# Mamba-2 scan and maxout FFN on one core: output products of five chunks in 512 columns and turned on VectorE, masks in 32x32 tiles, a new order

## The chip, the cores and the metric

The kernel runs on one core of one Trainium2 chip. The metric is the device time of one execution in microseconds (us). The kernel before was timed three times; where one figure is given, it is the median.

## The reference

A state-space scan with decay feeds a feed-forward layer whose activation is the largest of three products. All data are float32.

```python
# x (4, 8, 768, 32)   a (4, 8, 768)   B, C (4, 8, 768, 16): batch, head, position, ...
log_a = np.log(np.clip(a, 1e-06, 1.0))
for c in range(768 // 32):
    cum = np.cumsum(la, axis=-1)                       # la: log_a of these 32 positions
    L = np.exp(cum[:, :, :, None] - cum[:, :, None, :]) * causal
    y_intra = np.einsum('bhij,bhjd->bhid', np.einsum('bhin,bhjn->bhij', Cc, Bc) * L, xc)
    y_inter = np.einsum('bhin,bhnd->bhid', Cc, state) * np.exp(cum)[:, :, :, None]
    y[:, :, sl] = y_intra + y_inter
    state = decay_full * state + sum_j(B_j x_j * decay_from_j)
# bridge: (batch, head, position, 32) -> (batch * position, head * 32) = (3072, 256)
h = np.maximum(np.maximum(x @ w1, x @ w2), x @ w3)      # w1, w2, w3 (256, 768)
return h @ w_out                                        # w_out (768, 256)
```

## The kernel before

**Chunks.** The 768 positions are cut into six chunks c of 128; a chunk has its four batches side by side, so an activation tile has 512 columns (tokens), and 128 rows of features. The scan of a chunk needs the state left by the chunk before. All of it is in SBUF; weights and inputs are loaded once.

**Steps and the order.** The program is a table of some 1,500 named steps. Each belongs to an engine (t TensorE = PE, v VectorE = DVE, a ScalarE = ACT, p GpSimd = POOL, s SyncE = SP, whose steps are DMAs), lists the tiles it uses, and issues a few instructions. One hand-written string, `ORDER`, names the steps, `name` or `name/engine`; the program walks it once, so that on each engine the instructions stand in that order, and waits between engines follow from the tiles. A tile gets a slot of its pool at its first use and gives it back after its last. There are eight slots of PSUM (`ps`, one bank of 128x512 each).

**Precision.** A float32 product is taken as three products of parts, H·H, H·L and L·H (z = 0, 1, 2), where H is a rounded copy and L the rest. The weights are brought into a form for this by the steps `d` (load), `ab`, `lo`, `cl`, `sh`, `pl`, `sg`, `df`, and `h`/`l` with the name of a weight.

**The scan of a chunk.** `lB`, `lC` (loads of 32 KB) and `tB`, `tC` (32x32 transposes on DVE), or loads of 256 KB turned on PE (`trB`, `trC`), give B and C by state; `bt`/`tk` and `bk` turn B back. `s` are the products C·B, `left` and `right` are rows for the decay, and `e` or `em` multiplies them out: the exponent of L for a batch, 128 positions times eight heads of 64, one bank `e.c.b`. Of chunks 0 to 3 the causal mask is added in the same bank, by a matmul of a mask with an identity ahead of it (`mm.c.b`, `mask_mm`); `em` then accumulates onto it with two products of 32x64 tiles per batch. `xp` is the Exp into L, `w` the product with `s`, `yo` and `yw` the output y of the chunk, `A` and `S` the new state.

**The FFN of a chunk.** Chunks 0 and 1 take w1, w2, w3 in `up` steps (six matmuls of 512 columns each), with `m` and `h` for the maximum. The pairs of chunks (2, 3) and (4, 5) share products by the steps `q1` to `q7` on four banks E, F, G, H, with `x1`, `g7`, `e2`, `mx`, `hb`, `c1`, `c2`, `ha` and more around them. Either way there are six tiles of activations h (f = 0 to 5) per chunk, in parts `hH` and `hL`. Two more terms `y0`, `y1` come from y itself by a folded weight `fo`.

**The output.** A chunk's output is the sum of 24 steps `dn.c.term.z`: term h0 to h5, y0, y1, times z. Each is four matmuls, one for each batch b: the weights are the 128 tokens of the batch out of the activation tile, and 256 columns of w_out (`wo`) stream past. They add up in two banks `o.c.0` and `o.c.1`, tokens on partitions and 256 output columns per batch. `ob.c.u` copies a bank to SBUF (u = 0 on DVE, u = 1 on ACT, unless the order names another), `st.c.u` stores it, 256 KB. Chunk 5's copies and stores are in halves.

**The names in the profile.** `L892` is the matmul of `dn`, L337 the mask, L358 the `e` products, L799 `up`, L818 `q`, L506 `s`, L530 `yw`, L453 the turning back `tk`, L407 the transposes `tB` and `tC`, L184 a copy on ACT, L186 one on DVE, L189 a two-operand instruction, L402 the 32 KB loads, L650 weight loads, L955 the stores.

Of the kernel before, what the change touches and what calls it, by code (L numbers as in the profile page):

```python
# [23 lines left out]
a.1/s ident sel4 ones warm.20 own d.04 ind warm.4 ident16 table rowsel anew a.0/a clip.0 a.2  # L24
ln.0 nind scan.0 lo.04 pt0.0 pd1.0 mask mm.1.0 mm.0.0 ab.04 warm.21 pt1.0 left.0 clip.1 ln.1
mm.0.2 spread.0 warm.19 minus1 minus0 clip.2 esel En.0 d.12 warm.17 scan.1 ltC.0 pt0.1 lt.0
pd1.1 warm.11 ab.12 d.14 spread.1 mm.0.1 warm.8 cl.04 sh.04 cl.12 warm.13 warm.5 em.0.0 ln.2
scan.2 pt0.2 parity pd1.2 lo.12 lx.0 d.24 lt.1 mm.0.3 pt1.1 left.1 right.1.0 xp.0.0 d.22 sh.12
pl.12 E.0 em.0.1 xp.0.2 trC.0 cq.0.0 xp.0.3 trB.0 cpB.0 pt1.2 right.1.1 left.2 cq.0.1 xp.0.1
bd.0 ce.0 s.0 right.1.2 ab.14 cl.14 warm.18 sh.14 ltC.1 w.0.3 lo.14 w.0.2 d.02 warm.9 lo.24  # L30
En.3 warm.0 A.0 w.0.1 En.1 pl.14 ab.24 warm.10 w.0.0 lx.1 S.0.1 warm.16 d.11 lB.5.2 sg.14
sg.12 E.1 lB.2.2 lB.3.1 pl.04 lB.3.2 yw.0.0 S.0.0 yo.0 yw.0.1 mm.1.3 sg.04 E.3 cl.24 yH.0.1.1
d.10 mm.1.1 yH.0.0.1 yH.0.1.0 mm.1.2 yH.0.0.0/v yL.0.0.0 warm.23 right.2.1 right.2.0 ab.22
lC.4.7 df.04/v lC.5.6 trB.1 sh.24 yL.0.1.0 h.up04 d.00 lo.22 yL.0.1.1 right.2.2 yL.0.0.1 cl.22
l.up04/v em.1.0 xp.1.0 bt.2 cpB.1 xp.1.1 so.0.1 sa.0.1 sh.22 h.b4 pl.24 sg.24 ab.02 lC.3.3
trC.1 cq.1.0/v ce.1 lC.3.6 cq.1.1 En.2 em.1.1 lB.2.3 xp.1.3 pl.22 xp.1.2 l.b4 up.0.5.0 cl.02
df.24/v sh.02 bd.1/v up.0.4.0 E.2 sg.22 h.up24 s.1 m.0.4 w.1.1 d.01 d.21 so.1.0 lo.02 lC.2.1
A.1 S.1.0 mm.2.1 w.1.3 w.1.2 lB.2.5 l.up24 w.1.0 m.0.5 ab.11 lC.2.6 sa.1.0 warm.3 lB.2.7
up.0.4.1 mm.2.2 h.0.4 lC.3.5 yo.1 lB.4.1 S.1.1 pl.02 df.22 mm.2.3 sg.02 lC.2.0 right.3.0
h.up22 l.up22 df.02/v h.up02 l.up02 yw.1 yH.1.0.0/v up.0.5.1 yH.1.0.1/v yL.1.0.1 d.20 em.2.1  # L40
yH.1.1.1/v up.0.2.1 right.3.1 yH.1.1.0/v ab.01 lC.2.5 lC.5.0 yL.1.1.1 lB.3.3 xp.2.2 up.0.2.0
cl.11 ab.10/v lC.2.2 cl.10 lo.01 lB.2.0 yL.1.1.0 yL.1.0.0 up.1.4.0 lo.21 lC.2.3 ab.00 cl.00
xp.2.3 sh.00 ab.21 lo.11 sh.11 mm.3.0 lo.00 sw.2.0 sw.2.1 h.0.5 pl.11 sg.11 lC.4.5 mm.3.3
sh.10 sw.4.0 lo.10 mm.2.0 pl.00 ab.20/v pl.10 sw.4.1 sw.4.3 cl.01 mm.3.2 sg.10 em.2.0 m.0.2
sg.00 up.1.4.1 xp.2.1 lo.20 sh.01 xp.2.0 m.1.4 up.1.2.0 up.1.5.0 m.1.5 sw.2.2 h.0.2 h.1.4
df.00/v cl.20 sh.20 up.1.2.1 d.o2 pl.01 bt.1 sg.01 m.1.2 so.1.1/v pl.20 right.4.2 lC.2.7 h.b2
sg.20 h.up00/v lo.o2 lC.5.7 mm.3.1 l.up00 lC.2.4 df.20/v h.up20 up.0.3.0 lB.2.4 m.0.3
right.3.2 lB.2.6 em.3.1 em.3.0 d.o4 lB.2.1 l.up20 tC.2 cm.2.0 up.0.0.0.1 xp.3.0 cl.21 sh.21
pl.21 ab.o2 l.b2 up.0.3.1 tB.2 lC.4.2 sa.1.1 sg.21 xp.3.1 lC.3.4 lB.4.7 cl.o2 cm.2.1 xp.3.3
up.0.0.0.0 h.0.3 lB.3.6 tk.2 hH.0.3 h.1.2 bk.2 up.1.0.0 df.01/v d.o0 df.21 h.up21 l.up21/v  # L50
bt.0 ab.o4 lB.5.7 s.2 m.1.0 sw.2.3 lB.3.4 h.b0 lC.3.1 m.0.0 lo.o4 lB.5.3 sw.1.0 sh.o2 xp.3.2
up.0.0.1.0 up.0.0.1.1 so.2.0/v w.2.0 h.up01 w.2.1 lC.3.0 lx.2 up.1.5.1 pl.o2 sg.o2 sw.4.2
ab.o0 cd.2 h.1.5 w.2.2 hH.0.2 lC.3.2 hL.0.2 w.2.3 l.up01 cl.o0 cl.o4 sh.o4 sw.0.2 up.1.3.0
lt.3 sh.o0 lo.o0 A.2 pl.o0 up.1.3.1 S.2.0 h.wo2 lB.3.7 hH.1.2 m.1.3 S.2.1 sa.2.0 h.ss2 h.1.3
up.1.1.0 l.b0 pl.o4 l.wo2/v up.0.1.0 sw.0.0 lC.3.7 yo.2 m.1.1 sg.o0 up.1.1.1 sg.o4 hH.0.4
m.0.1/v h.0.0 lB.5.6 h.wo0 l.wo0 tC.3 cm.3.0 yw.2 yS.2.1.0 yS.2.1.1 lC.4.1 hH.1.5/v lC.5.2
h.wo4/v fold.2 lB.3.0 hH.0.5 fold.0 dn.0.h5.0 l.wo4 dn.0.h4.1 yS.2.0.1/v fold.4 right.5.1
yH.2.1.0 yH.2.1.1 bd.3 yL.2.1.1 hH.0.0 h.1.1 yS.2.0.0 yL.2.1.0 dn.0.h5.1 so.2.1/v hL.0.3
right.5.0 lB.4.2 h.fo dn.0.h2.1 hH.1.3/v yH.2.0.1 lB.3.5 tB.3 l.fo yL.2.0.1 dn.0.h0.1
# [964 lines left out]
```

## Time and profile before

| | |
|---|---|
| three runs | 239.13, 237.35, 238.9 us; median 238.9 us |
| span of the profiled execution | 236.7 us (its own time is not recorded apart; the median stands 2.2 us above its span) |
| PE | busy 221.5 us, 94% of the span, 3020 matmuls |
| DVE | busy 185.1 us, 78% |
| ACT | busy 98.6 us, 42% |
| POOL | busy 88.3 us, 37% |
| DMA | 17.49 MB in 71,051 packets, mean 74 GB/s; read 13.76 MB, written 3.15 MB |
| chain that ended last | PE 75%, DMA 9%, SP's queue 6%, ACT 4%, DVE 3% |

The span runs from the first to the last instruction of the profiled execution; the chain is the sequence of work and waits that ended last, followed back from the end. A matmul's busy time includes its way through the array, so that matmuls in a row overlap, and the pace of a row is read from its starts or from the length of many.

### The profile page before, as it was taken

How to read it: one execution, taken by the hardware profiler on the slowest of the kernel's cores; microseconds unless marked ns; L12 is line 12 of the kernel's file. 1: busy time of each engine (PE TensorE's matmuls, PEld its weight loads, DVE VectorE, ACT ScalarE, POOL GpSimd, SP SyncE). 2: the span in 40 equal slices, each digit the busy share in tenths (PEclk: the TensorE clock that was granted, in tenths of full speed). 3: DMA queues.
4: the chain of work that ended last, by engine and by line, in shares of the span. 5: the costliest groups of instructions: out<-in, count | busy, mean ns of one | idle time of the engine just before them, and what ended most of it. 6: DMA issues, size and time to landing. Idle time of an engine off the chain costs nothing.

```text
span 236.7 us, 7069 instructions
## 1 busy us (share of the span) xinstructions
PE 221.5 (94%) x3020; PEld 182.3 (77%) x3020; DVE 185.1 (78%) x340; ACT 98.6 (42%) x196; POOL 88.3 (37%) x85
## 2 busy tenths in 40 slices
...
GB/s 165 171 193 165 190 148 133 115 96 207 192 104 47 93 52 3 6 61 0 96 141 103 47 3 0 7 4 3 0 130 5 0 0 3 0 0 3 0 127 142
DMA packets 71051, 17.49 MB, mean 74 GB/s; under 512 B 63724, under 2 KB 68588, under 8 KB 71020
## 3 DMA queue, kind: packets, MB, share of 16 engines
...
q8 instruction: 24, 0.39, 0.8%
...
q14 instruction: 7, 0.06, 0.1%
HBM read 13.76 MB, written 3.15 MB: 71 GB/s over the span
## 4 chain that ended last, share of the span: by engine, by line
PE 75%; DMA 9%; SPq 6%; ACT 4%; DVE 3%; issue 1%; ACTq 0%; DVEq 0%
PE o L892 30%; PE E L818 11%; PE u L799 9%; DMA raw<-in_moe_w_dram 7%; PE G L818 6%; PE H L818 3%; PE F L818 3%; PE y L530 2%; SPq L650 2%; SPq L332 2%; PE s L506 2%; PE fold L768 2%; PE y L518 2%; DMA rawB<-in_B_dram 2%; PE A L491 1%
## 5 line engine op out<-in xcount | busy, mean ns | idle before, releaser
L189 POOL TENSOR_TENSOR u<-u,r 128x512 uint32<-128x512 uint32 (+1 forms) x12 | 12.8, 1075 | 25.1 <-DVE u L660 20.5
L189 POOL TENSOR_TENSOR hL<-x,hH 128x512 fp32r<-128x512 f32 x6 | 8.3, 1397 | 35.0 <-PE G L818 14.6
L385 ACT ACTIVATE L<-e 128x512 f32<-128x512 f32 x24 | 13.8, 595 | 6.7 <-PE e L358 6.7
L189 DVE TENSOR_TENSOR L<-s,L 128x512 f32<-128x512 f32 x24 | 15.5, 682 | 0.0
L184 ACT COPY x<-E 128x512 f32<-128x512 f32 x11 | 6.4, 586 | 16.1 <-PE E L818 15.8
L184 ACT CAST hH<-x 128x512 fp32r<-128x512 f32 x9 | 5.5, 625 | 16.8 <-DVE x L860 16.8
L189 POOL TENSOR_TENSOR hL<-h,hH 128x512 fp32r<-128x512 f32 x8 | 11.5, 1460 | 2.6 <-PE fold L768 1.3
L189 DVE TENSOR_TENSOR yL<-y,yH 128x256 fp32r<-128x256 f32 x24 | 9.6, 417 | 3.4 <-ACT yH L184 2.2
L189 DVE TENSOR_TENSOR x<-F,x 128x512 f32<-128x512 f32 x12 | 8.1, 686 | 5.0 <-PE F L818 5.0
L189 DVE TENSOR_TENSOR g<-E,g 128x512 f32<-128x512 f32 x12 | 8.3, 691 | 4.8 <-PE E L818 4.3
L189 POOL TENSOR_TENSOR T<-yS,T 128x512 f32<-128x512 f32 x3 | 4.3, 1425 | 20.0 <-PE o L892 18.3
L530 PEld LDWEIGHTS y<-L,x 64*32 64x32 f32 x768 | 8.7, 105 | 2.9 <-issue 2.2
L530 PE MATMUL y<-L,x 64*32 64x64 f32 x768 | 10.1, 224 | 0.7 <-issue 0.7
L189 DVE TENSOR_TENSOR g<-H,g 128x512 f32<-128x512 f32 x12 | 8.2, 686 | 2.8 <-ACT g L184 1.6
L184 ACT CAST yH<-y 128x256 fp32r<-128x256 f32 x17 | 5.7, 393 | 10.7 <-DVE yS L186 8.0
L877 DVE SCALAR_TENSOR_TENSOR hL<-g,hH 128x512 fp32r<-128x512 f32 x12 | 9.1, 774 | 0.9 <-PE o L892 0.9
L184 ACT COPY yS<-y 128x256 f32<-128x256 f32 x13 | 4.3, 376 | 13.1 <-PE y L530 11.6
L186 DVE COPY ob<-o 128x512 f32<-128x512 f32 (+1 forms) x5 | 3.1, 636 | 8.0 <-ACT ob L184 6.9
L184 ACT COPY ob<-o 128x512 f32<-128x512 f32 (+1 forms) x9 | 4.3, 519 | 11.9 <-PE o L892 11.9
L365 POOL TENSOR_SCALAR_AFFINE_SELECT L<-L 64x1024 f32<-64x1024 f32 x8 | 9.1, 1149 | 0.2
L662 ACT ACTIVATE r<-raw 128x512 f32<-128x512 uint32 (+1 forms) x12 | 6.4, 562 | 5.6 <-DMA raw<-in_moe_w_dram 5.6
L506 PE MATMUL s<-CT,BT 32*64 32x128 f32 x384 | 7.3, 278 | 1.5 <-ACT CT L442 1.5
...
## 6 DMA issues: line engine op xcount, KB each, us to landing
...
```

What stands on the lines that cost most here:

```text
L184: nc.scalar.copy(out=to, in_=src)
L189: engines[e].tensor_tensor(out=to, in0=p, in1=q, op=op)
L332: lambda e, c=c, p=p: engines[e].dma_start(out=at("right%d" % (c % 2))[4 * p + 3::RT], in_=at("left")[p::4, c * P:(c + 1) * P]))
L365: nc.gpsimd.affine_select(out=part, in_=part, pattern=[[0, 2 * NH], [1, Q]], compare_op=ALU.is_ge, fill=0.0, base=0, channel_multiplier=-1)
L385: lambda e, c=c, b=b: nc.scalar.activation(at("L.%d" % c)[:, b], at("e.%d.%d" % (c, b)), AF.Exp))
L506: nc.tensor.matmul(out=at("s.%d.%d" % (c, r))[side(g), b], lhsT=at("BT.%d" % c)[rows(r), b, side(g)], rhs=at("CT2.%d" % c)[rows(r), b, :, ...
L530: nc.tensor.matmul(out=at("y.%d.%d.%d" % (c, t, g))[q * D:(q + 1) * D, b], lhsT=at("x.%d" % c)[side(g), b * NH + h], rhs=at("L.%d" % c)[si ...
L662: step("lo." + name, "a", "%s %s" % (raw, r), lambda e: nc.scalar.activation(at(r).bitcast(FP32), word(0), AF.Copy, bias=2.0, scale=2.0 ** ...
L799: nc.tensor.matmul(out=o, lhsT=w[:, k, cols], rhs=v, start=(z == 0 and k == 0), stop=(z == 2 and k == KD - 1), skip_group_check=True)
L818: nc.tensor.matmul(out=at(bank), lhsT=w("HLH"[z]), rhs=y("HHL"[z]), start=(first and z == 0), stop=(z == 2), skip_group_check=True)
L877: nc.vector.scalar_tensor_tensor(out=at("hL." + df), in0=at("g7." + cf), scalar=0.0, in1=plain(at("hH." + df)), op0=ALU.max, op1=ALU.subtr ...
L892: nc.tensor.matmul(out=at("o.%d.%d" % (c, b // 2))[:, b % 2], lhsT=left[:, b * P:(b + 1) * P], rhs=right, start=(first and b % 2 == 0), st ...
```

## The change

**Output.** For chunks 0, 1, 2, 3 and 5 the steps `dn` become `dt`. The weights are now 128 of the 256 output columns of w_out (every second one: k = 0 the even, k = 1 the odd), and the 512 tokens of the activation tile stream past: two matmuls of 512 columns in place of four of 256. Banks `o.c.0` and `o.c.1` then hold output columns on partitions and tokens along the row. `ot.c.k` on DVE turns a bank in blocks of 32x32 into the tile `ot.c`, the two k interleaved. `su.c.b.q` stores one batch and one quarter of the output columns, 32 KB in pieces of 256 bytes: sixteen DMAs on SP for a chunk in place of two of 256 KB. Chunk 4 keeps `dn`, in 48 half steps, and its copies and stores become four of half the size.

**Masks.** A constant `edge` is made on POOL. For chunks 1, 2 and 3 the steps `mm` and `em` become `et`: for each batch the mask is added by four matmuls of 32x32 tiles, then the two of `em` follow.

**Order.** The string `ORDER` is a new one. The explicit `table` step, which loads ACT's function table, stood near the head and stands near the end now; the compiler puts a load of its own ahead of the first Ln and the first Exp. Many steps on ACT, DVE and POOL change their engine.

```diff
+    fixed("edge", [P, 2, Q], BF16)
...
+    def c_edge(e):
+        nc.gpsimd.memset(at("edge"), 0.0)
+        for r in range(NB):
+            nc.gpsimd.affine_select(
+                out=at("edge")[rows(r)], in_=at("edge")[rows(r)], pattern=[[-RT, 2], [1, Q]],
+                compare_op=ALU.is_ge, fill=MASKED, base=0, channel_multiplier=-1)
...
+    def edge_mm(c, b):
+        for g in range(2):
+            for t in range(2):
+                q = g * Q + t * RT
+                nc.tensor.matmul(
+                    out=at("e.%d.%d" % (c, b))[q:q + RT],
+                    lhsT=at("ident16")[rows(b), b * RT:(b + 1) * RT],
+                    rhs=at("edge")[rows(b), t].unsqueeze(1).to_broadcast([RT, NH, Q]),
+                    start=True, stop=False, tile_position=(b * RT, q), skip_group_check=True)
...
+            step("et.%d.%d" % (c, p), "t", es + need + " ident16 edge", lambda e, c=c, p=p: [
+                f(c, b, *m) for f, m in ((edge_mm, ()), (e_mm, (True,)))
+                for b in (2 * p, 2 * p + 1)])
...
-                rhs=right, start=(first and b % 2 == 0), stop=True, skip_group_check=True)
+                rhs=right, start=(first and b == bs[0]), stop=True, skip_group_check=True)
+
+    def spread_mm(c, term, z, ks):
+        n = int(term[1])
+        if term[0] == "y":
+            right = at("y%s.%d" % ("HHL"[z], c))[:, n]
+            left = at("fo" + "HLH"[z])[:, n]
+        else:
+            right = at("h%s.%d.%d" % ("HHL"[z], c, n))
+            left = at("wo%d" % (n // 2 * 2) + "HLH"[z])[:, n % 2]
+        for k in ks:
+            nc.tensor.matmul(
+                out=at("o.%d.%d" % (c, k)).rearrange("p a m -> p (a m)"),
+                lhsT=left[:, k::2],
+                rhs=right, start=((c, k) not in begun), stop=True, skip_group_check=True)
+            begun.add((c, k))
...
+        tmp("k4", "ot.%d" % c, [P, BLK // RT, RT, 2])
+        for k in range(2):
+            step("ot.%d.%d" % (c, k), "v", "ot.%d:%d o.%d.%d" % (c, k, c, k),
+                 lambda e, c=c, k=k: nc.vector.transpose(
+                     out=at("ot.%d" % c)[:, :, :, k],
+                     in_=at("o.%d.%d" % (c, k)).rearrange("p a (t j) -> p (a t) j", j=RT)))
+        for b in range(NB):
+            for q in range(NB):
+                step("su.%d.%d.%d" % (c, b, q), "s", "ot.%d" % c, lambda e, c=c, b=b, q=q:
+                     engines[e].dma_start(
+                         out=out[b * S + c * P:b * S + (c + 1) * P,
+                                 q * 2 * RT:(q + 1) * 2 * RT]
+                         .rearrange("(t j) m -> j t m", j=RT),
+                         in_=at("ot.%d" % c)[rows(q), b * NB:(b + 1) * NB]
+                         .rearrange("j t i k -> j t (i k)")))
```

Of `ORDER`, the end before and now:

```diff
-ob.2.0 st.2.0 st.5.0.0 dn.4.h2.1 dn.4.h3.2 st.5.1.0 dn.4.h2.2 dn.4.h1.0 st.5.0.1 dn.4.h4.2
-ob.4.0/a ob.4.1 st.4.0 st.4.1
+dn.4.h3.2.1 dn.4.y1.1.1 dn.4.h4.2.1 ob.4.1.0 su.2.3.0 ob.4.0.1 st.4.0.1 st.4.0.0 ob.4.1.1/v
+st.4.1.0 st.4.1.1
```

How it moves instructions is shown at three places. The first is the head of ACT's instructions: `la` are the inputs a (L299, then L315, is the Ln on them), `raw` weight words, L385, then L414, the Exp. Before:

```order
L219 ACT_TABLE_LOAD
L293 DMA la_98<-in_a_dram 128x1x128
L293 DMA la_101<-in_a_dram 128x1x512
L299 ACTIVATE la_98<-la_98 128x128
L662 ACTIVATE r_108<-raw_81 128x512
L652 ACTIVATE u_126<-raw_81 128x512
L299 ACTIVATE la_66<-la_66 128x128
L184 COPY right_142<-nind 128x1024
L184 COPY right_144<-nind 128x1024
L652 ACTIVATE u_170<-raw_154 128x512
L299 ACTIVATE la_101<-la_101 128x512
L662 ACTIVATE r_203<-raw_154 128x512
```

And now, on the same engine from its first instruction:

```order
L309 DMA la_66<-in_a_dram 128x1x128
L309 DMA la_94<-in_a_dram 128x1x512
L315 ACT_TABLE_LOAD
L315 ACTIVATE la_66<-la_66 128x128
L191 CAST t_0_131<-cum_125 128x128
L681 ACTIVATE u_139<-raw_77 128x512
L315 ACTIVATE la_90<-la_90 128x128
...
L471 ACTIVATE CT_0_201<-trC_180,parity 128x4x128
L414 ACT_TABLE_LOAD
L414 ACTIVATE L_207<-e_2_171 128x512
```

The table load that stood first stands behind two DMA issues, a second one stands ahead of the first Exp, and one of the two weight passes (L662) has left ACT there.

The second place is PE just ahead of `tk`, which turns the BT of chunk 2 back; `u_f` are banks of `up`. Before:

```order
L358 MATMUL e_1_1028<-right_142,left 64x512
L799 MATMUL u_0_0_1066<-yH_482,up00H 128x4x64 x2
L799 MATMUL u_0_0_1066<-yH_482,up00L 128x4x64 x2
L799 MATMUL u_0_0_1066<-yL_493,up00H 128x4x64 x2
L799 MATMUL u_3_1_1082<-yH_482,up22H 128x512 x2
L799 MATMUL u_3_1_1082<-yH_482,up22L 128x512 x2
L799 MATMUL u_3_1_1082<-yL_493,up22H 128x512 x2
L453 MATMUL tk_1110<-ident,BT_1089 128x128 x4
```

Now:

```order
L828 MATMUL u_2_1_1163<-yH_432,up22H 128x512 x2
L828 MATMUL u_2_1_1163<-yH_432,up22L 128x512 x2
L828 MATMUL u_2_1_1163<-yL_500,up22H 128x512 x2
L828 MATMUL u_0_0_1172<-yH_870,up00H 128x512 x2
L828 MATMUL u_0_0_1172<-yH_870,up00L 128x512 x2
L828 MATMUL u_0_0_1172<-yL_895,up00H 128x512 x2
L828 MATMUL u_1_0_1179<-yH_432,up01H 128x512 x2
L828 MATMUL u_1_0_1179<-yH_432,up01L 128x512 x2
L828 MATMUL u_1_0_1179<-yL_500,up01H 128x512 x2
L482 MATMUL tk_1192<-ident,BT_1123 128x128 x4
```

Whole `up` steps of both chunks, those on the weights `up00` and `up01` among them, stand ahead of `tk` where the products of the mask and halves of `up` stood.

The third place is the end of DVE: `o` is an output bank, `hL`, `hH`, `x`, `e` belong to the activations of the last pair. Before:

```order
L189 TENSOR_TENSOR hL_3_3379<-x_4_3_2880,hH_3_3139 128x512
L189 TENSOR_TENSOR e_4_1_3209<-G_1_3116,e_4_1_3209 128x512
L860 SCALAR_TENSOR_TENSOR x_4_1_3188<-e_4_1_3209,x_4_1_3188 128x512
L189 TENSOR_TENSOR hL_4_3461<-x_4_4_2903,hH_4_3214 128x512
L186 COPY ob_0_3463<-o_0_3090 128x256
L186 COPY ob_0_3483<-o_0_3061 128x512
```

Now:

```order
L196 TENSOR_TENSOR e_4_0_3122<-G_0_2985,e_4_0_3122 128x512
L889 SCALAR_TENSOR_TENSOR x_4_0_3103<-e_4_0_3122,x_4_0_3103 128x512
L998 STREAM_TRANSPOSE ot_3259<-o_1_3033 128x512
L998 STREAM_TRANSPOSE ot_3259<-o_0_3032 128x512
L196 TENSOR_TENSOR hL_0_3339<-x_4_0_3103,hH_0_3277 128x512
L193 COPY ob_0_3373<-o_0_3182 128x256
L193 COPY ob_1_3381<-o_1_3230 128x256
```

Two transposes of chunk 2's output stand between the last maximum and the last low part, where a copy of a bank stood at the very end.

More of the change, by code (lines that the diff above doesn't have):

```diff
@@ L23 @@
 ORDER = """
[L24 to L59, printed above, removed]
```

153 lines of the change are left out of this document (101 added, 52 removed).

## The prediction

> **What bounds the kernel now.** I read the head of the page first, then the engines stage by stage, then the chain of work that ended last.
>
> ```profile
> span 236.7 us, 7069 instructions
> ...
> PE 221.5 (94%) x3020; PEld 182.3 (77%) x3020; DVE 185.1 (78%) x340; ACT 98.6 (42%) x196; POOL 88.3 (37%) x85
> ...
> PE 75%; DMA 9%; SPq 6%; ACT 4%; DVE 3%; issue 1%; ACTq 0%; DVEq 0%
> ```
>
> TensorE is busy for 94% of the span and holds 75% of the chain; VectorE, which gets the new work, has 51.6 us to spare over the whole span. Whether it has any where it is needed is told by the stages (a line for each: from and to, length, then the busy time of PE, weight loads, DVE, ACT and POOL with the count of instructions, the granted clock, the DMA share and GB/s).
>
> ```profile
> 15.80:64.70 48.90, 42.82 (x790) 30.87 (x794) 42.89 (x91) 28.88 (x59) 24.45 (x25) 1.00 0.73 155
> 64.70:94.60 29.90, 29.90 (x658) 25.94 (x666) 26.96 (x53) 14.28 (x30) 16.81 (x15) 1.00 0.47 62
> 94.60:129.60 35.00, 35.00 (x359) 30.60 (x359) 29.45 (x44) 14.14 (x29) 21.51 (x17) 1.00 0.55 69
> 129.60:162.70 33.10, 32.84 (x625) 27.15 (x629) 27.88 (x50) 9.64 (x20) 8.35 (x9) 1.00 0.04 11
> 162.70:188.00 25.30, 25.30 (x250) 21.24 (x250) 21.53 (x36) 10.84 (x24) 5.66 (x4) 1.00 0.10 32
> 188.00:232.00 44.00, 44.00 (x331) 42.18 (x329) 23.78 (x36) 9.38 (x18) 8.34 (x6) 1.00 0.06 19
> ```
>
> `s.2` starts at 64.7, `s.4` at 129.6 and `yw.5`, the last of the scan's products, at 162.7. Up to 64.7 nothing is full (PE idle 6.1 of 48.9 us). From 64.7 on PE has no idle time to speak of, and a microsecond off PE is a microsecond off the kernel as long as DVE follows. DVE is busy 26.96 + 29.45 + 27.88 = 84.3 of the 98.0 us between 64.7 and 162.7: that is the stretch where it could become the bound. After 162.7 it has 24 us to spare. The granted clock is 1.00 throughout.
>
> What holds the front is seen in the chain (start, us, what):
>
> ```profile
> 27.33 7.82 DMA raw<-in_moe_w_dram
> ...
> 56.80 4.09 DMA rawB<-in_B_dram
> ...
> 62.88 1.38 PE u L799 x6
> ```
>
> Weights first, later the B of chunk 2, then an `up` step on PE. BT, the transpose of that B, costs PE this in the list of waits:
>
> ```profile
> PE tk L453 <- DVE BT L407: 1.4, 1, 1.4
> ```
>
> **The change part by part**, against the profiled execution's own end (236.7 us of span; the median of the three runs is 238.9, so 2.2 us lie around the span, which I leave alone).
>
> *Output products (T1).* 120 steps `dn`, four matmuls of 256 columns each, become 120 steps `dt`, two of 512.
> The chain has 512- and 256-column matmuls, each with a weight load of its own, in long rows:
>
> ```profile
> 122.16 2.05 PE G L818 x9
> ...
> 169.72 2.07 PE E L818 x9
> ...
> 210.55 21.49 PE o L892 x179
> ```
>
> 256 columns take 21.49/179 = 0.120 us (four 0.480), 512 take (2.05 + 2.07)/18 = 0.229 (two 0.458). The columns streamed are the same; what goes is 0.022 to 0.024 us a step, and 120 x 0.023 = **-2.8 us**, all of it where PE is full. The `dt` weights are every second column of a tile. No row shows a load with such a step. From the rows of unit step, a load is hidden behind a matmul of 0.120; if the stepped one took twice that, 0.24, since it spans twice the bytes, it would pass the 0.23 of its matmul, a step would cost 0.48 again, and T1 would be 0. I take -2.8, nearest to the rows that there are.
>
> *Masks (T2).* In chunks 1 to 3 twelve 128x128 mask matmuls go; their six pairs of `em` become `et`, each with eight 32x32-tile matmuls of 512 columns added.
>
> ```profile
> 35.32 0.39 PE L337 MATMUL e<-mask,ident 128*128 128x512 bf16 x1
> 35.55 0.38 PE L963 MATMUL warm<-ones 128*128 128x512 bf16 x1
> ...
> 42.58 0.41 PE L358 MATMUL e<-right,left 32*64 32x512 bf16 x4
> 42.92 0.73 PE L799 MATMUL u<-yH,up22H 128*128 128x512 f32 x2
> ...
> 56.99 0.42 PE L358 MATMUL e<-right,left 32*64 32x512 bf16 x8
> 57.34 0.50 PE L799 MATMUL u<-yH,up00H 128*128 128x256 f32 x2
> ```
>
> A mask costs 35.55 - 35.32 = 0.23, twelve 2.8. Eight tiles of 32x64 took 0.35 (56.99 to 57.34), and four took 0.34: they run side by side. No row shows 32x32 tiles. If all eight ran beside the four that follow, they would cost nothing (-2.8); if the four of one row strip ran one after another, 4 x 0.23 = 0.92 a step, 5.5 in all (+2.7). I take the row of eight, 0.35: 6 x 0.35 - 2.8 = **-0.7**. `edge` costs POOL five instructions, once, in the front where POOL is idle half the time.
>
> *The order around s.2 (T3).* The last DMA of chunk 2's B is row 48 of SP's queue where it was row 58, and six and a half more `up` steps stand ahead of `s.2`: 6.5 x 1.38 (the row at 62.88) = 9.0 us of PE work that doesn't need chunk 2. So PE's wait for BT should go: **-1.4**; at worst it stays, 0. The 9.0 us themselves are moved, not saved. But PE idles 6.1 us between 15.8 and 64.7, and 4.7 of that are other waits (for weights, `x`, CT). If earlier weight loads let the moved steps fill them, up to 4.7 more go. I take 0 of it, since DVE is busy 42.89 of the same 48.9 us and decodes the same weights, and keep the 4.7 for the range.
>
> *VectorE (T4).* Ten transposes come in; of DVE's five output copies two short ones stay.
>
> ```profile
> L407 DVE STREAM_TRANSPOSE CT<-rawC 128x512 f32<-128x512 f32 x4 | 4.5, 1125 | 0.0
> ...
> L186 DVE COPY ob<-o 128x512 f32<-128x512 f32 x4 | 2.7, 690 | 1.2 <-PE o L892 1.1
> ```
>
> These transposes read SBUF; the new ones read PSUM and write every second element, which no row shows. A copy from PSUM takes 0.69 for the same tile; I take 1.1 each, 11 us in all. Between `s.2` and `yw.5` the new list holds four transposes (+4.4) against two copies (-1.4), while what else comes to DVE there (`cm`, `bd`, `T`) and goes (`h`, decoding) is about even: 84.3 + 3.0 = 87.3 us. PE loses the 9.0 us moved ahead and gets 64 `dt` for 63 `dn` (29.4 for 30.2) and one more `q` step (0.7): 98.0 - 9.0 - 0.8 + 0.7 = 88.9. DVE at 87.3 against PE at 88.9 leaves almost nothing: PE will wait now and then for an `h`, a `bt` or a bank that `ot` has yet to empty. I put **+1** on it; 0 at best, and the rival below has the worst. Ten banks are held 0.4 us longer each (1.1 against 0.69); at worst 4 us, if each were waited for.
>
> *Start and table loads (T5).* The combined table load at the head is replaced by two that the compiler places, ahead of the first Ln and of the first Exp; the listed one comes late.
>
> ```profile
> 0.80 1.28 ACT L219 ACT_TABLE_LOAD   x1 [0.80 <-PEq L1008]
> ```
>
> One more in the front is 1.28 us of ACT ahead of the first `xp`; ACT is busy 28.88 of 48.9 us there, and the chain is on the weights' DMAs. I take **0**, with 1.3 as the upper end. The late one falls between ACT's waits for PE. The Trainium skill, "ScalarE: Activation LUTs", section "What ACT_TABLE_LOAD costs", adds a drain of 1380 ns to the 1283 ns of the load, 2.66 us per switch; the trace agrees on the load (1.28 us) and shows no second switch, and by the page T5 would be at most 2.7.
>
> *Tail (T6).* Eighty 32 KB stores replace ten of 256 KB, and all stand on SP.
>
> ```profile
> 43.06 0.43 SPq L402 DMA_DIRECT2D rawB<-in_B_dram  x1
> 43.54 0.42 SPq L402 DMA_DIRECT2D rawC<-in_C_dram  x1
> ...
> 232.06 1.07 ACT L184 COPY ob<-o 128x512 f32<-128x512 f32 x2 [4.12 <-PE o L892]
> ```
>
> SP issues the like-shaped 32 KB loads 0.48 us apart, so chunk 2's sixteen take 7.6 us. Behind chunk 2's last product stand 44 half steps `dn.4` of 0.24, 10.6 us; two transposes of 1.1 and the hand-overs off it, `ot.2.0` ends about 7.8 us ahead of PE's end: SP is just through when chunk 4's four quarter stores come. These are copied in halves on two engines, where 1.07 us of ACT follow PE now (up to -0.7), but four issues of 0.48 stand in one row (up to +1.5). I take **+0.3**.
>
> Sum: -2.8 - 0.7 - 1.4 + 1 + 0 + 0.3 = -3.6, and 238.9 - 3.6 = **235.3 us**.
>
> **The rivals.**
>
> *The front gives more.* The 4.7 us of idle time fill with the moved `up` steps: 230.6. For it: weights d.01, d.00, d.20 are issued earlier. Against it: DVE there.
>
> *DVE becomes the bound (slower).* Its 13.7 us of waits in the 98.0 are mostly for PE, such as
>
> ```profile
> DVE x L189 <- PE F L818: 5.0, 4, 3.1
> ```
>
> If PE is late for DVE as often as now, these stay on top of 87.3: 101.0 in place of 89.9 (88.9 and T4), that is 235.3 + 11.1 = 246.4. If PE runs ahead, they shrink. Each us of them beyond 2.6 costs one; the kernel is slower than 241.3 from 8.6 us on. Against it: the `up` steps are out of the stretch, and ACT and POOL both lighter, so that the operands of DVE come sooner.
>
> *The saving is cancelled.* Stepped weights gain nothing: 235.3 + 2.8 = 238.1. Or 32x32 tiles run one after another: 235.3 + 3.4 = 238.7. Or all ten banks are waited for: 239 with T4's one counted in. Or the stores are slow: their pieces are 256 bytes, as those of the `rawB` loads, which landed in 4.09 us (row at 56.80). If SP, with sixteen in a row, waited for landings so that an issue took 0.75 instead of 0.48, chunk 2's sixteen would take 12 us, and 4 us would stick out: 239.3. The Trainium skill, "DMA: Bandwidth & Descriptors", section "Specifications", speaks against the change here: below 512 bytes a transfer misses line rate and is done as read-modify-write. The trace has such pieces only as loads.
>
> **How the numbers follow.** No change means within 1%, 236.5 to 241.3, about what a measurement of this kernel can tell. Forecast (233 to 236.5): 0.40. More from the front (under 233): 0.19. Cancelled: 0.27. DVE bound or several at once (over 241.3): 0.14. So faster 0.59, same 0.27, slower 0.14. The range leaves out the far end of the slow rival and a little below the good one: 230.5 to 240.5.
>
> **What would show it.** T1: rows of `o` matmuls at 0.23 us apiece; 0.24 or more says that the loads bind. T2: from an `et` step to the next, 0.7 us (0.35 and the old 0.34); 1.3 says one after another. T3: no wait of `tk` for BT. T4: DVE under 90 us between `s.2` and `yw.5` and PE's idle time there under 5; DVE full and PE waiting for `h`, `T` or `ot` says the slow rival. T5: two table loads in the first 30 us, off the chain. T6: under 5.5 us from the last PE matmul to the end; SP stores 0.75 apart say slow stores. I am wrong in kind if PE's idle time after `s.2` exceeds 10 us.

## The result: slower by 3.5%

The changed kernel takes 248.47 us (median of four runs, 245.08 to 250.56) against 238.91 before; the ratio of the two is 1.035 [1.026, 1.044]. Here and below a time is the median of all runs of a kernel, while a ratio leaves out the runs that lie over 1.5% above the kernel's fastest (here 249.24 and 250.56). Its profiled execution took 247.69 us with a span of 245.6, so 2.1 us lie around the span, as before.

The head of its page, with the granted clock in 40 slices:

```profile
span 245.6 us, 6721 instructions
...
PE 223.7 (91%) x2816; PEld 176.8 (72%) x2816; DVE 196.5 (80%) x359; ACT 91.5 (37%) x179; POOL 92.0 (37%) x90
...
PEclk9957559999999988997999999999999999999998
...
PE 74%; DVE 11%; issue 7%; POOL 4%; DMA 2%; ACT 1%; DVEq 0%; POOLq 0%
```

Two things are new: "issue" holds 7% of the chain where it held 1%, and the clock is not full: 5 to 7 tenths in the front, and dips later. The stages, cut at `s.2`, `s.3`, `s.4`, `yw.5` and PE's end (columns as in the prediction's table):

```profile
78.80:101.40 22.60, 20.36 (x461) 17.66 (x460) 19.31 (x40) 7.82 (x17) 8.02 (x10) 0.92 0.04 9
101.40:147.70 46.30, 44.35 (x439) 35.08 (x438) 39.91 (x64) 15.95 (x30) 27.01 (x22) 0.96 0.33 47
147.70:174.30 26.60, 25.06 (x559) 20.43 (x559) 24.68 (x46) 7.07 (x16) 3.36 (x4) 1.00 0.23 36
174.30:241.60 67.30, 67.30 (x463) 57.51 (x459) 47.39 (x80) 16.93 (x32) 9.65 (x7) 1.00 0.11 26
```

Set against the prediction's steps (starts of the steps on PE, us; the forecast for a stage is the sum of its terms there, with T2 put wholly into the third row; these rows add up to -3.3, the prediction's rounded terms to -3.6):

| stage | before | after | forecast | measured |
|---|---|---|---|---|
| to the start of `s.0` | 15.8 | 17.4 | 0 | +1.6 |
| `s.0` to `s.1` | 16.5 | 20.7 | 0 | +4.2 |
| `s.1` to `s.2` | 32.3 | 40.7 | +6.9 (9.0 moved in, T2, T3) | +8.4 |
| `s.2` to `yw.5` | 98.0 | 95.5 | -8.1 (9.0 moved out, T1, T4) | -2.5 |
| `yw.5` to PE's end | 69.6 | 67.3 | -2.4 (T1, one `q` less) | -2.3 |
| PE's end to the end | 4.5 | 4.0 | +0.3 | -0.5 |

The loss is in three places: 5.8 us before `s.1`, 1.5 between `s.1` and `s.2`, and 5.6 between `s.2` and `yw.5`. In the list of waits the last two have a name:

```profile
PE y L559 <- issue: 7.3, 4, 2.0
```

Before, this was 0.7 us. Of the four, one of 1.8 us stands in `yw.1`, ahead of `s.2` (with 0.8 more in `yo.1`), and 5.5 us stand in `yw.2`, `yw.3` and `yw.4`. In the timeline of PE such a wait is a hole inside `yw`, and what follows it runs at half pace (start, length, count; the last bracket is the idle time ahead):

```profile
86.76 0.76 PE L559 MATMUL y<-L,x 64*32 64x64 f32 x55
89.49 0.99 PE L559 MATMUL y<-L,x 64*32 64x64 f32 x71 [1.97 <-issue]
...
91.43 1.05 PE L797 MATMUL fold<-wo2L,b2H 128*128 128x256 f32 x4
92.28 1.05 PE L797 MATMUL fold<-wo2H,b2L 128*128 128x256 f32 x4
...
93.87 0.64 PE L797 MATMUL fold<-wo4L,b4H 128*128 128x256 f32 x4
94.35 0.64 PE L797 MATMUL fold<-wo4H,b4L 128*128 128x256 f32 x4
```

`yw` stops after 55 of its matmuls for 1.97 us. Four `fold` matmuls then take 0.85 us (91.43 to 92.28) where they take 0.48 later (93.87 to 94.35). The windows tell why, in the last columns but two:

```profile
90.00:94.00 4.00, 4.00 (x56) 3.88 (x47) 2.24 (x6) 1.00 (x3) 0.73 (x1) 0.57 0.01 4
94.00:98.00 4.00, 4.00 (x29) 3.74 (x28) 3.18 (x7) 2.27 (x6) 1.42 (x2) 1.00 0.01 2
```

A mean clock of 0.57 in 4 us is 3.4 us at half speed: by an estimate from that, this wait of 2 us costs up to 1.7 more behind it. The Trainium skill, "TensorE: Matmul & The Clock Gate", Part 1, has the clock set in fixed windows of 3413 ns by how busy PE was in them; the 3.4 us agree.

What does the wait wait for? In the DMA view of the changed kernel from 86 to 90 us, one packet is all that moves:

```profile
DMA packets 1, 0.02 MB, mean 4 GB/s; under 512 B 0, under 2 KB 0, under 8 KB 0
...
q8 instruction: 1, 0.02, 1.8%
```

It has 16,384 bytes, and the trace holds 22 packets of this queue for 5,671 records of PE (weight loads, matmuls, semaphores), that of the kernel before 24 for 6,087: one for every 256. Counted over these records, each wait for instructions of 0.3 us or more, in this and all later traces, stands at a number 193 above a multiple of 256 (or one or two records behind it). How long the 256 instructions before it took, and the wait there (from the start of the block's last instruction to that of the next), for all blocks of under 5 us:

| kernel | block of 256 took -> wait, us |
|---|---|
| after | 1.39 -> 2.06; 1.47 -> 2.18; 1.55 -> 2.16; 1.62 -> 1.76; 3.27 -> 0.98; 3.70 -> 0.11; 4.63 -> 0 |
| before | 3.37 -> 1.09; 3.98 -> 0; 4.00 -> 0; 4.27 -> 0; 4.45 -> 0; 4.51 -> 0.47; 4.96 -> 0.63 |

A block used up in well under 3.5 us is followed by a wait that fills it up to about that. The packet shows what the time goes to: the block that ends in the hole begins at 85.84, its packet starts at 86.86 and ends at 87.99, and PE goes on at 89.49. All 20 traces agree. At none of their 433 ends of blocks did PE go on sooner than 1.20 us after the end of the block's packet (one for one, in order), and at the 60 where it waited over 0.3 us, it went on 1.24 to 1.83 us after it. So PE waits for this packet. `yw` alone is 256 instructions in 1.4 us. In the kernel before, no block had less than 3.37 us.

### The profile page after: what moved, and what is told of

It is laid out like the page before. It is cut to its first block, busy times and chain, and to the rows that moved or that the text cites. A ratio compares the mean times of both kernels' runs of the same rounds, so it can differ in the third digit from the quotient of the medians.

```text
span 245.6 us, 6721 instructions
## 1 busy us (share of the span) xinstructions
PE 223.7 (91%) x2816; PEld 176.8 (72%) x2816; DVE 196.5 (80%) x359; ACT 91.5 (37%) x179; POOL 92.0 (37%) x90
## 4 chain that ended last, share of the span: by engine, by line
PE 74%; DVE 11%; issue 7%; POOL 4%; DMA 2%; ACT 1%; DVEq 0%; POOLq 0%
PE o L934 24%; PE E L847 10%; PE G L847 7%; PE u L828 5%; PE o L921 5%; PE y L559 4%; PE F L847 3%; PE H L847 3%; PE y L547 3%; PE fold L797 2%; PE s L535 2%; DMA la<-in_a_dram 2%; PE A L520 1%; POOL u L686 1%; PE e L384 1%
## 5 line engine op out<-in xcount | busy, mean ns | idle before, releaser
L196 POOL TENSOR_TENSOR u<-u,r 128x512 uint32<-128x512 uint32 (+1 forms) x12 | 14.1, 1176 | 20.4 <-DVE u L689 15.1
L559 PE MATMUL y<-L,x 64*32 64x64 f32 x768 | 11.8, 232 | 7.9 <-issue 7.3
L414 ACT ACTIVATE L<-e 128x512 f32<-128x512 f32 x24 | 13.8, 603 | 4.9 <-PE e L384 4.9
L196 POOL TENSOR_TENSOR hL<-x,hH 128x512 fp32r<-128x512 f32 x3 | 4.5, 1503 | 26.7 <-ACT hH L191 13.5
L191 ACT CAST hH<-x 128x512 fp32r<-128x512 f32 x7 | 4.3, 628 | 21.4 <-DVE x L889 15.6
L191 ACT COPY g<-G 128x512 f32<-128x512 f32 x10 | 5.8, 595 | 14.5 <-PE G L847 14.5
L196 POOL TENSOR_TENSOR hL<-h,hH 128x512 fp32r<-128x512 f32 x6 | 7.6, 1286 | 8.2 <-DVE ss L196 3.5
L196 POOL TENSOR_TENSOR S<-S,old 128x256 f32<-128x256 f32 x5 | 4.3, 866 | 16.2 <-DVE S L196 9.5
L196 DVE TENSOR_TENSOR e<-G,e 128x512 f32<-128x512 f32 x12 | 8.0, 683 | 2.9 <-PE G L847 2.9
L686 POOL TENSOR_SCALAR u<-u 128x512 f32<-128x512 f32 (+1 forms) x6 | 9.3, 1560 | 0.3 <-DVE u L683 0.2
L196 POOL TENSOR_TENSOR old<-S,E 128x256 f32<-128x256 f32 x6 | 4.6, 764 | 12.8 <-DVE S L196 12.6
L998 DVE STREAM_TRANSPOSE ot<-o 128x512 f32<-128x512 f32 x10 | 6.7, 696 | 3.0 <-PE o L934 3.0
L535 PEld LDWEIGHTS s<-CT,BT 32*64 32x64 f32 x384 | 6.5, 144 | 3.6 <-ACT BT L191 1.8
```

What stands on the lines that cost most here:

```text
L191: nc.scalar.copy(out=to, in_=src)
L196: engines[e].tensor_tensor(out=to, in0=p, in1=q, op=op)
L414: lambda e, c=c, b=b: nc.scalar.activation(at("L.%d" % c)[:, b], at("e.%d.%d" % (c, b)), AF.Exp))
L535: nc.tensor.matmul(out=at("s.%d.%d" % (c, r))[side(g), b], lhsT=at("BT.%d" % c)[rows(r), b, side(g)], rhs=at("CT2.%d" % c)[rows(r), b, :, ...
L559: nc.tensor.matmul(out=at("y.%d.%d.%d" % (c, t, g))[q * D:(q + 1) * D, b], lhsT=at("x.%d" % c)[side(g), b * NH + h], rhs=at("L.%d" % c)[si ...
L686: step("cl." + name, "v", u, lambda e: engines[e].tensor_scalar(out=at(u).bitcast(FP32), in0=at(u).bitcast(FP32), scalar1=SMALL, scalar2=L ...
```

## The experiments

Each kernel was timed beside the kernel before, whose medians lay between 237.8 and 238.3; the ratio is to that.

**e1 to e3: warm-up matmuls, and large matmuls between yo and yw.** In e1 eleven `warm` steps are added to the order (ahead of `mm.0.1`, `En.0`, `em.0.1` and `s.0`). e2 moves a step or more in between:

```diff
-up.0.4.1 h.0.4 m.0.5/v yo.1 yw.1
+yo.1 up.0.4.1 h.0.4 m.0.5/v yw.1
...
-up.0.1.1 S.2.1 yo.2
+S.2.1 yo.2 up.0.1.1
...
-A.3 yw.2
+yw.2 A.3
...
-yo.3 yw.3
+yo.3 dt.0.h3.1 dt.1.h4.1 dt.1.y0.2 yw.3
...
-yo.4 hM.3.2 sa.4.1 yw.4
+yo.4 dt.3.h2.0 dt.3.y0.1 hM.3.2 sa.4.1 yw.4
```

e3 has both.

> The changed kernel with eleven more warm-up matmuls (512 columns, on a bank of their own) on PE ahead of the waits of its first 17 us; nothing else moves. Clock theory: the granted clock, which is 0.50 from 11.9 to 22 us and from 25.8 to 35 us in the changed kernel, is 1.00 before 20 us and stays there; s.2 starts near 72 us in place of 78.8, and the kernel takes 240 to 242 us in place of 247.7. DVE theory (VectorE holds the front and the middle): the clock rises but s.2 stays near 78 us, and the time stays at 246 to 249.

> The changed kernel with matmuls of 512 columns (an up step or two to three dt steps) moved in between yo and yw of chunks 1 to 4, where nothing or an A step stood. Instruction-supply theory (some 400 small instructions in a row outrun what feeds PE its instructions): the waits of yw put down to 'issue', 7.3 us in four, fall to under 2 us, the clock's two drops at 90 and 114 us go too, and the time falls by 5 to 9 us, to 239 to 243. Rival (the waits are put down wrongly and are for DVE or ACT): the waits stay or reappear under another name, time 246 to 249.

> Both edits together. If the two causes are separate: 232 to 236 us, the time forecast for the change. If VectorE is the bound behind them: not below 241.

e1: 249.21, ratio 1.045 [1.037, 1.053]. The clock was full from 7 to 17 us, then fell three times, for 3.4, 6.8 and 10.2 us; waits for instructions grew to 10.8 us. The extra matmuls gained nothing. e2: 244.41, 1.027 [1.020, 1.034]. Its list of waits has

```profile
PE y L557 <- issue: 1.2, 3, 0.5
```

and `s.2` to `yw.5` took 91.4 us in place of 95.5: 4.1 of the 5.6 us that were missing there, with no dip of the clock after 36 us. The interval of e2's time overlaps that of the changed kernel, and its trace is of its fastest run (242.86 us), so the stage shows the gain more surely than the total does. e3: 244.86, 1.029 [1.023, 1.035], no better than e2. The sum of both at 232 to 236 was wrong: the front did not get shorter but longer (`s.1` at 40.5, in e2 at 38.1).

**e4: unit step in the weights of dt.**

```diff
-                lhsT=left[:, k::2],
+                lhsT=left[:, k * P:(k + 1) * P],
```

> As e3_both, with the weights of dt taken as 128 neighbouring columns in place of every second one, so that the output's columns come out in another order (the output differs from the reference in that alone). Stepped-load theory: a dt step takes 0.457 us in place of 0.467, its weight loads about 105 ns in place of 207, and the kernel gains 1 us, hardly more than can be measured. Rival (0.467 has another cause, such as the change of bank at each matmul): 0.467 stays.

244.25, 1.024 [1.017, 1.031], against e3's 1.029: not told apart by time. The rows tell (chain and grouped lines; of e3 first, then of e4):

```profile
207.53 4.67 PE o L933 x20
L933 PEld LDWEIGHTS o<-hL,wo0H 128*128 128x128 f32 x20 | 3.9, 194 | 0.8
```

```profile
206.51 4.53 PE o L933 x20
L933 PEld LDWEIGHTS o<-hL,wo0H 128*128 128x128 f32 x20 | 3.8, 188 | 0.8
```

4.67/20 = 0.2335 us a matmul with every second column, 0.2265 with neighbours. The stepped load is longer by 6 ns, not by the 100 expected, and a `dt` step takes 0.467 in place of 0.453. (The 207 ns of the expectation were read off the changed kernel, where two of the 20 loads of a row fell into the half clock from 114.2 us on and took 330.)

**e5, e6: yo and yw side by side, and no warm-up, in the kernel before.**

```diff
-yo.2 m.1.1 sg.o0 up.1.1.1 sg.o4
+up.1.1.1 yo.2 m.1.1 sg.o0 sg.o4
```

The same is done with `dn.0.h2.0` at `yo.3` and `q6.2.2` at `yo.4`; e6 drops all sixteen `warm` steps.

> The kernel before, with the one step of large matmuls that stands between yo and yw of chunks 2, 3 and 4 moved ahead of yo, so that 64 and 128 small matmuls follow each other; nothing else. Instruction-supply theory: waits of yw put down to 'issue' grow from 0.7 us to 3 to 6 us, and the kernel to 241 to 246 us, the clock dropping behind some of the waits. Rival (the waits in the changed kernel have to do with its other edits): 237 to 240 us.

> The kernel before without its 16 warm-up matmuls; nothing else. Clock theory: the granted clock is 0.50 for 10 to 20 us of the first 40, and s.1 and s.2 start 3 to 8 us later, 241 to 246 us. Rival (the front is held by VectorE and the loads whatever the clock): s.2 within 1 us of 64.6, time 237 to 240.

e5: 237.17, 0.998 [0.996, 1.001]: no waits of `yw` at all. So which steps follow which is not enough to make the wait. e6: 237.25, 0.996 [0.992, 0.999]: without any warm-up matmul the kernel before lost nothing. That is not because its clock was full. The 0.999 on record counts the time ahead of the first clock record as full, and in e6 that record comes at 29.4 us; the rows of `yw.0.1` (e6, then the kernel before) show half pace until then:

```profile
25.38 1.93 PE L525 MATMUL y<-L,x 64*32 64x64 f32 x64
```

```profile
23.33 1.10 PE L530 MATMUL y<-L,x 64*32 64x64 f32 x64
```

`s.1` came 2.1 us later than before, `s.2` 1.9 us earlier: in the old order the way to `s.2` leads over the loads of weights (in the prediction's rows of the chain) and takes back what PE loses ahead of `s.1`. Both theories had to be changed: to the blocks counted above, and away from the warm-up steps.

**e7, e16: the new output alone, in the kernel before** (chunks 0 to 3 in e7; 0, 1 and 3 in e16), `dn`, `ob`, `st` replaced by `dt`, `ot`, `su` where they stood:

```diff
-SLOTS = {"k1": 16, "k2": 50, "k4": 12, "k8": 2, "ps": 8}
+SLOTS = {"k1": 16, "k2": 50, "k4": 13, "k8": 2, "ps": 8}
```

> The kernel before with the new output for chunks 0 to 3 alone (96 steps dn become dt, eight transposes, 64 stores of 32 KB, a thirteenth slot for tiles of that size); the old order, masks and end. Part theory: 96 x 0.013 = 1.2 us off PE after 64 us, nothing else: 236 to 238. DVE theory: eight transposes at 0.70 in place of copies shared with ACT make VectorE late, 239 to 243.

> The kernel before with the new output in chunks 0, 1 and 3 alone (72 dt steps, six transposes, 48 stores), so that no small stores stand at the end, as chunk 2's sixteen did in e7. Part theory: 72 x 0.013 = 0.9 us less, 237 to 238. Rival (the transposes hold PE up): PE's end 1 us or more later than before, 239 to 241.

e7: 244.23, 1.027 [1.022, 1.032]. Most of it is in SP's timeline:

```profile
229.83 7.43 SPq L998 DMA_DIRECT2D out_dram<-ot  x16
237.31 2.43 SPq L1013 DMA_DIRECT2D out_dram<-ob  x5
```

PE ends at 233.4, 1.1 us later than before, but in the old order chunk 2's output comes last, and its sixteen issues keep chunk 4's stores until 237.3. e16, without them: 239.95, 1.007 [1.004, 1.011]. `s.2` to `yw.5` took 100.0 us, 2.0 more than before, with PE waiting 1.0 us for CT at `s.5` and 0.8 for x: in the old order the new output costs, though PE has less to do.

**e8: the new masks alone, in the kernel before** (each `mm.c.b` of chunks 1 to 3 dropped, `em.c.p` replaced by `et.c.p`, `edge` behind `mask`).

> The kernel before with the masks of chunks 1 to 3 as 32x32 tiles alone. Part theory: 6 x 0.34 - 12 x 0.23 = -0.7 us, not to be told from 238. Rival: the mask matmuls also kept the clock at 1.00 in the front, and without them it drops: 240 to 245.

239.72, 1.008 [1.005, 1.012]: neither -0.7 nor 240 to 245. Waits for instructions grew from 1.5 to 4.0 us in the trace; the two longest, of 1.4 and 0.7 us, stand behind blocks of 2.9 and 2.2 us.

**e9, e10: parts taken back in the new order.** e9 puts `mm` and `em` in the places of `et`; e10 besides puts `dn`, `ob` and `st` back, so that the order alone is left.

> The changed kernel with the old masks (128x128 mask matmuls and em) in the places of et; the new order and the new output stay. Sum of parts: +0.7 us on PE, 248 to 249.5. Instruction-supply theory: 48 small matmuls and as many weight loads fewer in the front are worth more than the 0.7, 245 to 247.5.

> The new order with the old masks and the old output (dn, copies, two stores of 256 KB per chunk; a 51st slot for tiles of 2 KB); what is left of the change is the order, the places of the loads and the table loads. If the order and what it does to the front and to yw is the loss: 246 to 250. If the new output is (e7 lost 1 us in PE's own end with it): 238 to 243.

e9: 241.95, 1.009 [1.005, 1.014]. e10: 243.66, 1.024 [1.016, 1.031]. So in the new order the masks in 32x32 tiles cost 2.5% (1.035 to 1.009), and the new output gains 1.4% (1.024 to 1.009; the intervals nearly touch, and by the medians of all runs it is 0.7%); the order itself costs 2.4%. In e9's trace `s.0` to `s.1` took 18.2 us and `s.2` to `yw.5` 90.8; PE's demand there differs by under 1 us from the changed kernel's. What differs is the waits for instructions (5.1 us in all against 8.1), the time at half clock after 24 us (3.4 us against 17), and `edge`, which e9 doesn't make: in the changed kernel a weight step of POOL stands behind it, and VectorE waits for that step,

```profile
DVE u L689 <- POOL u L686: 1.1, 1, 1.1
```

which e9 doesn't show.

**e11 to e15: the head, and a clock held by force.** e11 is e2 with

```diff
-a.0/a ones ident sel4 d.12 warm.19 warm.21 own rowsel a.1/s warm.18 a.2
+table a.0/a ones ident sel4 warm.19 warm.21 own rowsel a.1/s warm.18 a.2 d.12
...
-ot.5.1 table su.5.2.2
+ot.5.1 su.5.2.2
```

for which these rows of ACT's timeline of the changed kernel gave the reason (Ln stood at 3.79, Exp at 11.44 before):

```profile
5.55 0.31 ACT L315 ACTIVATE la<-la 128x128 f32<-128x128 f32 x1 [2.18 <-DVE la L312]
...
12.07 1.28 ACT L414 ACT_TABLE_LOAD   x1
13.36 0.60 ACT L414 ACTIVATE L<-e 128x512 f32<-128x512 f32 x1
```

e12 adds eight warm-up matmuls around `A`, `yo` and `yw` of chunk 0; e13 adds eighteen instead, in one bank of their own; e14 is e11 with the old masks and without `edge`; e15 is e14 with the eighteen.

```diff
+        step("hd.%d" % n, "t", "hold ones", lambda e, n=n: [nc.tensor.matmul(
+            out=at("hold"), lhsT=at("ones"),
+            rhs=at("ones").unsqueeze(1).to_broadcast([P, NB, P]), start=True, stop=True,
+            skip_group_check=True) for _ in range(2)])
```

> As e2_between, with the table load first on ACT as in the kernel before, and weight load d.12 behind the loads of a. The Ln and Exp of the first chunk stood 1.8 and 1.9 us later in the changed kernel than before. If that carries on to the end: s.0 near 15.8 in place of 17.4 us, and 242 to 243.5 in place of 244.4. If something later holds the front: 244 to 245.

> As e11_head, with eight warm-up matmuls around the A, yo and yw of chunk 0 (21 to 26 us), where the clock fell to 0.50 in the changed kernel while the chain stood on PE until 43 us. Clock theory: the clock stays at 1.00 between 22 and 36, s.1 starts near 34 in place of 38, and the time is 2 to 4 us below e11_head. Rival (clock losses in the front are hidden, as in the runs of the kernel before, whose times show nothing of a mean clock between 0.96 and 1.00): same as e11_head within 1 us.

> As e11_head, with eighteen warm-up matmuls between En.3 and the end of yw.0.1 (20 to 27 us), all in one bank of their own, so that none waits for VectorE as those of e12 did; nothing else. Clock theory: with PE busy the clock doesn't fall at 25 us, s.0 to s.1 takes 17 to 18 us in place of 21.4, and the time falls by 2 to 4 us against e11. Rival: s.0 to s.1 stays over 20 us whatever the clock does.

> The new order and output with the old masks, large matmuls between yo and yw of chunks 1 to 4, and the head of e11. If the losses found add up (7 us of waits and what follows them, the masks' small instructions, the head): 236 to 239. If they are one and the same loss: 240 to 243.

> As e14, with the eighteen matmuls of e13. Clock theory: 2 to 4 us below e14, below the kernel before. Rival: as e14.

| | us | ratio | `s.0` | `s.0` to `s.1` |
|---|---|---|---|---|
| e11 | 245.23 | 1.021 [1.014, 1.027] | 15.6 | 21.4 |
| e12 | 245.40 | 1.029 [1.025, 1.034] | 15.8 | 24.5 |
| e13 | 242.36 | 1.017 [1.012, 1.023] | 15.6 | 20.8 |
| e14 | 241.92 | 1.014 [1.008, 1.021] | 15.7 | 18.2 |
| e15 | 242.94 | 1.022 [1.017, 1.027] | 15.7 | 19.3 |

e11 brings `s.0` back to 15.6 and gains nothing: what was won there was lost before `s.1`. e12's added matmuls waited for VectorE themselves (1.8 us), and the clock fell at 23 us. In e13 it did not; from 24 to 38 us the windows of the changed kernel, e11 and e13 read

```profile
24.00:38.00 14.00, 13.67 (x216) 10.53 (x216) 11.03 (x21) 8.53 (x18) 6.65 (x6) 0.63 0.88 191
```

```profile
24.00:38.00 14.00, 14.00 (x256) 10.88 (x245) 10.91 (x21) 9.52 (x20) 6.52 (x7) 0.63 0.97 220
```

```profile
24.00:38.00 14.00, 13.45 (x348) 9.13 (x335) 10.09 (x21) 9.44 (x20) 6.63 (x7) 1.00 0.77 185
```

yet `s.1` came only 0.6 us earlier. Its chain shows where the rest went:

```profile
22.09 1.29 PE hold L1025 x6
...
24.17 0.54 PE hold L1025 x2
...
25.74 0.54 PE hold L1025 x2
...
26.90 0.54 PE hold L1025 x2
...
29.30 0.97 PE hold L1025 x4
```

3.9 us of fill stand in PE's own row; 20.8 - 3.9 = 16.9, next to the 16.5 of before. Holding the clock by matmuls costs as much as it saves, and no run of the new order has the front at full clock for nothing. But the traces lost it for different lengths of time. Cut at the first matmul of `yw.0`, in us:

| | `s.0` to `yw.0` | `yw.0` to `s.1` | of it at half clock | PE idle in it |
|---|---|---|---|---|
| before | 5.2 | 11.3 | 0 | 1.5 |
| e9, e14 (no `edge`) | 5.4, 5.4 | 12.8, 12.8 | 3.4 | 1.5 |
| e10 (no `edge`) | 5.4 | 14.3 | 6.8 | 1.5 |
| changed, e2 | 6.7, 6.7 | 14.1, 14.0 | 10.2 | 0.3 |
| e3, e4 | 6.7, 6.7 | 16.6, 16.2 | 13.7 | 1.8, 1.1 |

The second column less the idle time and half of the time at half clock is 8.0 to 9.8 us in every row, so from `yw.0` on the half clock is what makes the front long; the first column shows `edge`, 1.3 us. e14 doesn't add up to the 236 to 239 of its first theory: it is no better than e9. Its waits of `yw` fell to 1.5 us, but the blocks now end elsewhere: 1.5 us in `A`, 1.7 in the masks and exponents of the front, 4.7 in all against e9's 5.1.

**e17, e18: only the number of instructions.** 64 or 128 small matmuls are put into the kernel before, ahead of `En.0` and `s.0`:

```diff
+        step("tiny.%d" % n, "t", "tiny.%d ones" % n, lambda e, n=n: [nc.tensor.matmul(
+            out=at("tiny.%d" % n)[i % 4 * RT:(i % 4 + 1) * RT, 0:Q],
+            lhsT=at("ones")[side(n % 2), 0:RT], rhs=at("ones")[side(n % 2), 0:Q],
+            start=True, stop=True, tile_position=(n % 2 * Q, i % 4 * RT),
+            skip_group_check=True) for i in range(32)])
```

> The kernel before with 64 small matmuls on a spare bank (32 ahead of En.0, 32 ahead of s.0, where PE waits anyway), that is 128 more instructions on PE's queue, half of the 256 that one 16 KB load of instructions holds; nothing else. Page theory: in all traces so far PE's waits for instructions stand at the instruction whose number is 193 above a multiple of 256, and a block of 256 that is used up in less than 3.6 us is followed by a wait that fills it up to that. Shifted by 128, the blocks of the kernel before hold yo and yw whole: waits of 0.6 to 2 us in six places, 7.7 us by its own trace, some of them hidden; yw's waits put down to 'issue' 4 to 8 us, time 241 to 245. Rival (the numbers agree by chance, or the 64 matmuls themselves cost): as e18.

> As e17 with 128 small matmuls, 256 more instructions, a whole block, so that the blocks' bounds stand at the same steps again as in the kernel before. Page theory: no more waits than the kernel before, 238 to 239.5. Rival (the small matmuls cost by their number): twice what e17 loses.

e17: 240.06, 1.008 [1.004, 1.012]. e18, with twice as many: 238.64, 1.002 [0.998, 1.006]. The waits for instructions, of e17 and of e18:

```profile
PE y L526 <- issue: 3.1, 3, 1.8
```

```profile
PE s L502 <- issue: 2.0, 1, 2.0
PE trB L429 <- issue: 0.3, 1, 0.3
```

Half a block of 256 brings the waits of `yw`, a whole one takes them away again (the 2.0 us that are left stand at `s.0`, behind the 128 themselves). In e17 they are at number 193 above multiples of 256 once more, behind blocks of 1.95, 2.27 and 2.36 us. The place where the 16 KB blocks end is the cause of these waits; the size was forecast too high, 3.1 us of waits in `yw` and 1.9 us of time, not 4 to 8 and 3 to 7. By time alone e17 and e18 lie 1.4 us apart, with intervals that overlap at their ends.

## Why the prediction was wrong

**The step that failed first** is one that had no term: "PE has no idle time to speak of, and a microsecond off PE is a microsecond off the kernel as long as DVE follows". It took for granted that PE's instructions are there. The changed list of instructions puts `yo`, `A` and `yw` into blocks of 256 that are used up in 1.4 to 1.6 us, and PE waited 7.3 us in `yw` for the next, with two dips of the clock of 3.4 us behind that. The forecast between `s.2` and `yw.5` was -8.1 us; measured were -2.5, and -6.6 in e2, where the waits are gone. The "issue" row of the profile before (0.7 us) and e17 show that the kernel before has its blocks at steps where they don't hurt; the prediction shows the 1% of "issue" and gives it no term.

**"The granted clock is 1.00 throughout"** was the second: it held for the trace of the kernel before from 15.8 us on. In the changed kernel it is 0.50 for 10 us from 25.4 us on, where the chain is on PE without a gap:

```profile
24.63 1.23 PE y L559 x60
25.86 1.06 PE y L547 x32
26.92 1.86 PE y L559 x64
...
32.52 1.71 PE bt L786 x8
...
35.09 3.08 PE u L828 x12
```

`yw` with 64 matmuls takes 1.86 us here and 1.23 just before. Half of 10 us is 5; PE idled 1.2 us less than before, and `yw.0` to `s.1` grew by 2.8. The other 1.4 of the 4.2 us between `s.0` and `s.1` lie ahead of `yw.0`. The table above and the sum from e13 agree; no run changed the clock of the new order alone, so this rests on the rows of many traces. The same loss cost the kernel before nothing (e6): a low clock costs where PE is the chain. What made the clock fall at 25 us no run shows.

**T1** had the right mechanism and was mis-sized: a step gains 0.480 - 0.467 = 0.013, 120 of them 1.6 us, not 2.8. The stepped weights cost the rest (0.453 with neighbours, e4). In the new order the new output gained (e10 to e9), in the old one it lost (e16): part of its worth seems to lie in where the list puts the transposes, which no run moved alone.

**T2**: the row of eight was the right price,

```profile
62.52 0.41 PE L362 MATMUL e<-edge,ident 32*32 32x512 bf16 x8
62.86 0.41 PE L384 MATMUL e<-right,left 32*64 32x512 bf16 x4
63.20 0.41 PE L362 MATMUL e<-edge,ident 32*32 32x512 bf16 x8
```

0.34 us for the eight. But the sum counted PE's time and not its instructions: 72 more of them, which move all later blocks and are used up at 24 per 0.68 us. And `edge`, five instructions in a front "where POOL is idle half the time", was put at nothing: they stand ahead of a step that VectorE needs, and in the four kernels of the table that make it `yw.0` starts 1.3 us later behind `s.0`. The masks cost 0.8% in the old order and 2.5% in the new.

**T3** was right: no wait of `tk` for BT is left. The 4.7 us of idle time in the front gave nothing, as taken. **T4**: the transposes from PSUM are cheaper than those that the prediction went by,

```profile
L998 DVE STREAM_TRANSPOSE ot<-o 128x512 f32<-128x512 f32 x10 | 6.7, 696 | 3.0 <-PE o L934 3.0
```

0.70 us, not 1.1, and VectorE was busy 19.31 + 39.91 + 24.68 = 83.9 us of 95.5, not full. It was nearly full where the prediction gave it no term, between `s.1` and `s.2`: 36.5 of 40.7 us, with the chain on it and on POOL from 53 to 80 us, in the steps that bring the weights into parts (this is 7 of the 11% of DVE on the page):

```profile
38.10:78.80 40.70, 36.48 (x510) 27.91 (x509) 36.52 (x71) 21.00 (x44) 25.94 (x24) 1.00 0.66 126
```

```profile
60.10 1.20 DVE ss L196 x2
...
70.07 1.90 POOL u_o L686
71.99 1.29 DVE u_o L689 x2
```

This stretch took 39 us or more in every kernel of the new order, while in the old one it shrank from 32.3 to 28.4 when `s.1` came late (e6); so the new order has nothing there to make up for the front. **The slow rival** gave 246.4, near the 247.7 of the profiled execution, by the wrong mechanism, and the nearness is luck: behind `s.2` VectorE had 11.6 us to spare, and PE waited for instructions, not for it. **T5**: the start was 1.6 us later (the a behind d.12, the second table load), above the bound of 1.3, and no run separates the two, but e11 shows that it decided nothing. **T6** was close, 4.0 us from PE's end in place of 4.5, and the rival of slow stores fell:

```profile
224.52 16.84 SPq L1004 DMA_DIRECT2D out_dram<-ot  x32
241.45 1.84 SPq L1019 DMA_DIRECT2D out_dram<-ob  x4
```

16.84/32 = 0.53 us an issue with 256-byte pieces, and SP was through just as PE ended at 241.6.

Still open: how the 2.4% for the order alone (e10) divide. Its trace has 6.2 us of waits for instructions and 10.2 us at half clock behind 24 us, by rows enough for its loss of 6.5 us of span, but no run separates the two.
